# A new list order for a scheduled kernel: transposing DMAs earlier, some loads later

## The chip, the cores and the metric

The kernel runs on one NeuronCore of a Trainium2 chip. Its engines run side by side: PE (TensorE, matrix products, with PEld for loading weights), DVE (VectorE), ACT (ScalarE), POOL (GpSimd) and SP (SyncE, which here only issues DMAs). Sixteen DMA engines move data between HBM and SBUF, the on-chip memory; matrix products land in PSUM, which has eight banks of 128 x 512 float32. The metric is the device time of one execution in microseconds (us). The median of three runs of the kernel before was 200.03 us (198.92 to 200.92).

## What is computed

Two branches start from the layer norm of `x = A_q` (2048 tokens, 512 channels), and their product is added to x:

```
xn = layernorm(x)
# A: a long convolution over time, per channel, by FFT
k_shift = sum over t < 4 of k_pad[:, t:t+S] * shift_k[:, 3-t]
kv = k_shift * v
y  = irfft(rfft(pad(kv)) * rfft(pad(ssm_k)))[:S] + kv * ssm_D
s  = xn * y
# B: a gated feed-forward layer, 512 -> 1792 -> 512
h  = gelu(xn @ w_gate) * (xn @ w_up)
g  = silu(h @ w_down)
out = x + s * g
```

All tensors are bfloat16; the sums are float32.

## The kernel before

**The feed-forward branch.** The tokens are cut into four quarters q0 to q3 of 512. For each quarter the normalized rows XN are transposed to xnT (q0 and q1 on PE, q2 and q3 by a transposing DMA, line 846). Each of 14 column blocks m has a gate task (psg) and an up task (psu) of four matmuls of 128x512 each; ACT takes the gelu out of PSUM to GE (three buffers, L1137), and DVE multiplies it with the up product into HT (L1140). The down tasks (psd) multiply HT with Wd. Of q0, the blocks m = 0 and 1 go in two halves of 256 columns (L1128, L1130). The weights come as chunks g0 to g3 and u0 to u3, and Wd as Wd0 and Wd1.

**The convolution branch** is an FFT written as matrix products in two stages, with a trip to HBM between them. The filter ssm_k comes as Hn0 to Hn3. Hn0 and Hn1 are transposed on PE into HTr; Hn2 and Hn3 are first permuted by ACT (four HP copies, L609), and then the two halves HP0 and HP1 are transposed by DMA into HTD0 and HTD1 (L899). DVE adds ssm_D to one row of each (fold and foldD). Stage 1 of the filter multiplies HTr (H0 to H7) and HTD (J0 to J7) with the table F1; the results are evicted to the AST buffers, stored to HBM as ZH (H stores by ACT's queue, J stores by SP's) and loaded again as BH. Stage 1 of kv does the same: DVE makes k_shift out of the loads KK0 to KK4 and the taps SKB (which POOL copies out of SKR), chain kac and ktm, eight vector operations per quarter, the last one writing kv over V (L1005 to L1013); PE multiplies V with F1 (K0 to K7), and the evictions go through three AST slots to ZK and come back as BK. The second stage (32x32 tiles, L1028) works on BH and BK, DVE multiplies the two spectra (L1091), the inverse uses the tables MI0 and MI1 (made by ACT, m_turn at L729, and transposed by DMA at L1039), results go out as ZI, and the last y tasks read BI.

**What sets the order.** Every step is a task with a number; `S.add` gives it the engine (or a choice of two engines) and a planned duration. The string `SEQ` lists all 787 tasks in the order in which they are emitted, and a `b` behind a number takes the second engine. So each engine's instructions, and each queue's DMAs, stand in the order of that list, and each engine works in that order: what stands behind a waiting instruction on its engine waits too. Loads (planned as a queue of their own, `loads`) and the planner's `SP` tasks are both issued by SP, in one order. `Sched.run` walks the list with planned times; since order and engine are fixed by the list, its times only choose buffer slots: `Pool_.find` takes the slot of a pool (PSUM banks, AST, GE, HS, BO and so on) that is planned to be free first. `Trk` adds the semaphore waits that the data and the slots need.

Task numbers that the text uses:

| number | task | engine |
|---|---|---|
| 25, 26 | loads of Hn2, Hn3 | SP |
| 30, 28, 29, 37, 38 | loads of SKR, g2, u2, g3, u3 | SP |
| 35, 40, 44, 46 | loads of V0, V1, V2, V3 | SP |
| 43, 41, 42 | loads of KK3, Wd0, Wd1 | SP |
| 57, 58; 59, 60 | copies to HP0 out of Hn2, Hn3; to HP1 | ACT |
| 61, 62 | transposing DMAs to HTD0, HTD1 | SP |
| 64 | foldD | DVE |
| 81 | m_turn, which makes TFA and TFB | ACT |
| 122, 128, 129, 130 | J0's matmuls; J2's, its eviction, its store ZH10 | PE, PE, ACT, SP |
| 166 | first step of kac2, reads KK3 | DVE |
| 183, 184 | transposing DMAs to MI0, MI1 | SP |
| 252, 257 | K5's and K6's second matmul pair | PE |
| 406, 430, 409 | psu0_7, first reader of u2; psu0_13, a reader of u3; psg0_8 | PE |
| 433, 448 | first down tasks of rows 0 and 3 of q0 | PE |
| 467, 469 | transposes of XN5 and XN7 | PE |

Of the kernel before, what the change touches and what calls it, by code (L numbers as in the profile page):

```python
# [24 lines left out]
N_WARM = 11  # L25
ORDER = "x02 h0 h1 x22 w0 w1 h2 h3 D0 w2 s0 k0 v0 x1 w3 k1 v1 d0 d1 k2 v2 k3 v3 x2 x3"
SEQ = (
# [22 lines left out]
)  # L50
NF_BANKS = 4
ISSUE = 470.0
# [1 line left out]
W_XT, W_SW, W_BK, W_BH, W_ZI, W_BI, W_ZK, W_MI, W_G1 = 1665000, 600000, 555000, 703000, 333000, 640000, 490000, 740000, 222000  # L54
# [237 lines left out]
class Sched:  # L292
# [7 lines left out]
    SHARE_BW = 300.0  # L300
    FIRST = {"loads": 1050.0, "SP": 30500.0}
    DRAIN = 121.0
    EARLY, TAKEN, SHARED, WAIT = (0.0, 1.0), 1400.0, 46000.0, ((30000.0, 5000.0), (38000.0, 1500.0), (46000.0, 4500.0), (57000.0, 2000.0))
    LANDS = (4350.0, 5590.0, 6870.0, 8420.0, 9350.0, 10200.0)

    def __init__(self):
# [92 lines left out]
def build_kernel(nc, A_q, A_k, A_v, A_shift_k, A_ssm_k, A_ssm_D, B_w_gate, B_w_up, B_w_down, out):  # L399
    with ExitStack() as es0:  # L400
# [104 lines left out]
        S = Sched()  # L505
# [128 lines left out]
        bHP, bHTD = [[B(f"{x}{h}") for h in range(2)] for x in ("HP", "HTD")]  # L634
# [255 lines left out]
        h_perm, h_dtr = [], []  # L890
        d_htd = [dsem(f"d_htd{hf}") for hf in range(2)]
        for hf in range(2):
            for k in range(2):
                h_perm.append(op([("ACT", 2090.0)], lambda e, h, hf=hf, k=k: copy(e, h, HP[:, 8 * hf:8 * hf + 8, k, :], Hn[:, 2 + k, :].rearrange("p (a t) -> p t a", t=NT)[:, 8 * hf:8 * hf + 8, :]),
                                 r=[bHn[2 + k]], w=[bHP[hf]], rr=[R_Hn[2 + k]], ww=[R_HP[hf]]))
        for hf in range(2):
            def dtr(e, hf=hf):
                o = HTD[:, 8 * hf:8 * hf + 8, :, :].rearrange("p t k d -> p (t k) d")
                trk.dma("SP", lambda h: h.dma_start(out=o, in_=HP[:, 8 * hf:8 * hf + 8, :, :].rearrange("p t k a -> p (t k a)"), transpose=True), d_htd[hf], r=[R_HP[hf]], w=[R_HTD[hf]])  # L899
            h_dtr.append(S.add([("loads", 2900.0)], dtr, r=[bHP[hf]], w=[bHTD[hf]], nbytes=W_XT))  # L900
        HT0 = HTr[0:1, 0, :].rearrange("p (d c) -> p c d", c=2)[:, 0, :]
        HD0 = HTD[0:1, 0, :, :].rearrange("p k d -> p (k d)")
        bFold, bFoldD = B("fold"), B("foldD")
# [1 line left out]
           r=[bHD, *[bHTr[k][0] for k in range(2)]], w=[bFold], rr=[R_D, *R_HTr[0]], ww=R_HTr[0])  # L905
        op([("DVE", 420.0)], lambda e, h: h.tensor_tensor(HD0, HD0, Drow[:, 256:512], ALU.add),
           r=[bHD, bHTD[0]], w=[bFoldD], rr=[R_D, R_HTD[0]], ww=[R_HTD[0]])
# [315 lines left out]
        for j in range(6):  # L1223
# [7 lines left out]
                  r=[b2], w=[B(f"out{j}")], nbytes=262144)  # L1231
# [12 lines left out]
def bass_recurrent_scan__ssm_conv_h3__glu_gated_geglu__prompt_kernel(  # L1244
    nc: bass.Bass,
    A_q: bass.AP,
    A_k: bass.AP,
    A_v: bass.AP,
    A_shift_k: bass.AP,
    A_ssm_k: bass.AP,  # L1250
    A_ssm_D: bass.AP,
    B_x: bass.AP,
    B_w_gate: bass.AP,
    B_w_up: bass.AP,
    B_w_down: bass.AP,
    out: bass.AP,
):
    build_kernel(nc, A_q, A_k, A_v, A_shift_k, A_ssm_k, A_ssm_D, B_w_gate, B_w_up, B_w_down, out)
# [28 lines left out]
```

## Time and profile before

| | |
|---|---|
| median of three runs | 200.03 us |
| the profiled execution | 198.18 us |
| its span, first to last instruction | 196.4 us |
| PE busy in it | 188.6 us, 96% |
| DVE, ACT busy | 163.6 and 122.6 us |
| bytes moved | 49.19 MB, mean 250 GB/s |
| clock granted to PE | full speed throughout |

A row of the timeline has the start in us, the length in us, the engine (a q behind it means the engine's queue, which issues DMAs), the line, the operation, output and inputs, the shape and how many instructions were merged; the bracket is the idle time of the engine just before and what ended it. A row of the chain of waits has start, length and what was done. A row of the table by stage has the stretch, its length, for PE, PEld, DVE, ACT and POOL the busy time with the number of instructions, then PE's clock, the share of the DMA engines and GB/s. A row of the list of DMAs ends with the number of transfers, the size and the median time from issue to landing.

### The profile page before, as it was taken

To read this page: it belongs to the slowest core of one execution; us is meant where nothing else is said; L and a number is where in the kernel's file an instruction comes from. 1 tells how busy PE (TensorE), PEld (TensorE's weight loads), DVE (VectorE), ACT (ScalarE), POOL (GpSimd) and SP (SyncE) were. 2 spreads that over 40 slices of the span, in tenths; PEclk is the share of its full clock that TensorE was granted. 3 is DMA by queue.
4 is the path that set the end of the run, shared out by engine and by line. 5 is a ranking of instruction groups with operands and counts; after the bars stand their busy time and mean duration, and the time that the engine had idled before them with its cause. 6 is when DMAs were issued, how large, how long until landed. Compare 5 with 4: busy or idle time off the path is not lost.

```text
span 196.4 us, 3497 instructions
## 1 busy us (share of the span) xinstructions
PE 188.6 (96%) x1377; PEld 84.5 (43%) x1377; DVE 163.6 (83%) x249; ACT 122.6 (62%) x166; POOL 13.8 (7%) x32
## 2 busy tenths in 40 slices
PE   8899969999999999899999999999999999999993
PEld 2675425444444444334344343434333444444442
DVE  6799896999979997968689977958797986598993
ACT  5796596996988797767665655868775522430121
POOL 5322600000000000020210000000000000000000
PEclk9999999999999999999999999999999999999999
DMA  6999999199999999999999893958152433929443
GB/s 169 321 328 314 374 386 410 36 168 228 355 351 392 267 298 256 385 335 328 255 255 282 187 344 139 316 190 304 69 203 110 160 110 123 391 80 366 160 147 124
DMA packets 45958, 49.19 MB, mean 250 GB/s; under 512 B 12787, under 2 KB 39671, under 8 KB 45942
## 3 DMA queue, kind: packets, MB, share of 16 engines
q1 hardware_dynamic: 37366, 42.67, 69.7%
q10 hardware_dynamic: 8576, 6.29, 11.0%
q8 instruction: 11, 0.18, 0.4%
q14 instruction: 5, 0.04, 0.1%
HBM read 27.39 MB, written 14.68 MB: 214 GB/s over the span
## 4 chain that ended last, share of the span: by engine, by line
PE 65%; DMA 21%; ACT 7%; SPq 3%; issue 2%; DVE 1%; ACTq 0%
PE psall L618 60%; DMA Wu<-in_B_w_up_dram 8%; PE psall L1028 5%; DMA Wd<-in_B_w_down_dram 4%; DMA Wg<-in_B_w_gate_dram 4%; DMA ZK<-AST 3%; SPq L590 2%; DMA ZH<-X 2%; ACT X L609 2%; ACT GE L1137 1%; ACT HP L609 1%; ACT TFA L729 1%; ACT AST L609 1%; ACT TFB L729 1%; ACTq L590 0%
## 5 line engine op out<-in xcount | busy, mean ns | idle before, releaser
L618 PE MATMUL psall<-xnT,Wu 128*128 128x512 bf16 (+1 forms) x232 | 54.8, 372 | 1.9 <-DMA Wu<-in_B_w_up_dram 1.9
L618 PE MATMUL psall<-xnT,Wg 128*128 128x512 bf16 (+1 forms) x232 | 54.4, 372 | 0.1
L618 PE MATMUL psall<-Wd,HT 128*128 128x512 bf16 (+2 forms) x238 | 52.5, 367 | 0.3 <-DMA Wd<-in_B_w_down_dram 0.3
L1140 DVE TENSOR_TENSOR HT<-psall,GE 128x512 bf16<-128x512 f32 x54 | 36.7, 686 | 11.5 <-PE psall L618 11.5
L1137 ACT ACTIVATE GE<-psall 128x512 bf16<-128x512 f32 x54 | 30.9, 599 | 14.2 <-PE psall L618 10.6
L618 PEld LDWEIGHTS psall<-xnT,Wu 128*128 128x128 bf16 x232 | 21.9, 98 | 28.3 <-issue 2.2
L618 PEld LDWEIGHTS psall<-Wd,HT 128*128 128x128 bf16 x238 | 22.2, 98 | 26.7 <-issue 1.7
L618 PEld LDWEIGHTS psall<-xnT,Wg 128*128 128x128 bf16 x232 | 21.4, 98 | 25.6 <-issue 2.5
L609 ACT ACTIVATE HS<-psall 128x1024 bf16<-128x1024 f32 x14 | 13.9, 1024 | 6.0 <-PE psall L1028 6.0
L1011 DVE TENSOR_TENSOR KAC<-KAC,KTM 128x2048 bf16<-128x2048 bf16 x12 | 14.6, 1220 | 0.1
L1009 DVE TENSOR_TENSOR KTM<-KK,SKB 128x2048 bf16<-128x2048 bf16 x12 | 14.6, 1217 | 0.0
L609 ACT ACTIVATE KB<-psall 128x1024 bf16<-128x1024 f32 x11 | 11.1, 1026 | 5.7 <-PE psall L1028 5.7
L609 ACT ACTIVATE AST<-psall 128x1024 bf16<-128x1024 f32 x12 | 12.0, 1026 | 3.0 <-PE psall L618 2.9
L1172 ACT ACTIVATE G<-psall 128x512 bf16<-128x512 f32 (+2 forms) x5 | 2.6, 512 | 17.1 <-PE psall L618 17.1
L609 ACT ACTIVATE X<-psall 128x512 bf16<-128x512 f32 (+1 forms) x16 | 12.6, 819 | 0.7 <-PE psall L618 0.7
L1166 DVE SCALAR_TENSOR_TENSOR G<-G,psall 128x512 bf16<-128x512 bf16 x12 | 8.1, 682 | 5.7 <-ACT G L1164 5.7
L612 DVE CAST BO<-psall 128x1024 bf16<-128x1024 f32 x9 | 10.9, 1222 | 1.9 <-PE psall L1028 1.9
L1164 ACT ACTIVATE G<-psall 128x512 bf16<-128x512 f32 x12 | 6.8, 595 | 8.0 <-PE psall L618 8.0
L609 ACT ACTIVATE BO<-psall 128x1024 bf16<-128x1024 f32 x7 | 7.2, 1024 | 7.3 <-PE psall L1028 7.2
L821 DVE BATCH_NORM_STATS2 stats<-X 128x6 f32<-128x512 bf16 x16 | 10.5, 678 | 1.0 <-DMA X<-in_A_q_dram 1.0
L1091 DVE TENSOR_TENSOR HW<-KB,HW 128x1024 bf16<-128x1024 bf16 x16 | 10.9, 683 | 0.0
L1091 DVE TENSOR_TENSOR HS<-KB,HS 128x1024 bf16<-128x1024 bf16 x16 | 10.9, 684 | 0.0
(84 smaller groups left out, 176.3 us busy)
## 6 DMA issues: line engine op xcount, KB each, us to landing
BH<-ZH SPq DMA_DIRECT2D x8, 512.0 KB, 6.6
HW<-HS SPq DMA_DIRECT2D x16, 256.0 KB, 3.5
BK<-ZK SPq DMA_DIRECT2D x8, 512.0 KB, 5.1
ZI<-BO ACTq DMA_DIRECT2D x16, 256.0 KB, 2.5
BI<-ZI SPq DMA_DIRECT2D x8, 512.0 KB, 4.1
ZK<-AST SPq DMA_DIRECT2D x6, 512.0 KB, 5.3
Hn<-in_A_ssm_k_dram SPq DMA_DIRECT2D x4, 512.0 KB, 8.4
KK<-in_A_k_dram SPq DMA_DIRECT2D x4, 512.0 KB, 11.1
```

Source lines behind the costliest of these rows:

```text
L609: return h.activation(o, i, ACTF.Copy, scale=scale)
L612: return h.tensor_copy(o, i)
L618: return h.matmul(o, lhsT=l, rhs=r, start=st, stop=sp)
L821: t_stats[t] = op([("DVE", 670.0)], lambda e, h, t=t: h.bn_stats(stats[:, t, :], X[:, t, :]), r=[bX[q][t % 4]], w=[bst[t]], rr=[R_X[t]], w ...
L1009: op([("DVE", dur)], lambda e, h, j=j, m=m: h.tensor_tensor(KTM[:, m.slot, :, :], kk(j), sk(j), ALU.mult), r=need + [bSKB[j], a], w=[m], r ...
L1011: op([("DVE", dur)], lambda e, h, m=m: h.tensor_tensor(KAC[:, a.slot, :, :], KAC[:, a.slot, :, :], KTM[:, m.slot, :, :], ALU.add), r=[m], ...
L1028: trk.op("PE", lambda h: h.matmul(ps(s, i)[b, :], lhsT=wt(col)[a, :], rhs=data(col)[a, :], start=n < 16, stop=n >= len(todo) - 16, tile_po ...
L1091: return hd.tensor_tensor(o, flat(KB, kb[h]), o, ALU.mult)
L1137: op([("ACT", act(512))], lambda e, h: h.activation(GE[:, g.slot, :], bank(pg), ACTF.Gelu_apprx_tanh), r=[pg], w=[g], rr=lambda: R_bank(pg ...
L1140: op([("DVE", dve(512, 1))], lambda e, h: h.tensor_tensor(HT[:, q % 2, m, :], bank(pu), GE[:, g.slot, :], ALU.mult), r=[pu, g], w=[bHT[q][m]],
L1164: op([("ACT", act(n))], lambda e, h, g=g, pc=pc: h.activation(g, pc(), ACTF.Tanh, scale=0.5), r=[p], w=[bt], rr=lambda p=p: R_bank(p), ww= ...
L1166: op([("DVE", dve(512, 1))], lambda e, h, g=g, pc=pc: h.scalar_tensor_tensor(out=g, in0=g, scalar=1.0, in1=pc(), op0=ALU.add, op1=ALU.mult ...
```

## The change

No instruction is added or taken away. The list `SEQ` is replaced, with twelve evictions moved from DVE to ACT and eight from ACT to DVE; two planner constants and the planned duration of the two HTD transposes change.

```diff
 SEQ = (
-    "17 18 19 20 21 22 36 0 3 2 11 8 4 12 5 1 6 7 9 65 66 50 10 67 73 68 74 13 49 75 82 52b 112 107 51 76 113 83 87 86b 102 71 23 72 69 24 79 54 "
...
+    "0 2 3 1 17 5 18 19 8 7 11 50 4 9 12 10 65 13 49 6 66 73 67 68 51 74 52b 82 75 54 112 76 86b 83 20 117 56 21 87 71 53 118 72 119 102 69 70 79 "
+    "120 369 371 121 22 55b 377 77 370 80 85 78 379 84 372 89 14 93 88 103 36 23 24 378 107 113 108 114 380 373 31 459 25 30 375 381 455 460 15 "
...
-    EARLY, TAKEN, SHARED, WAIT = (0.0, 1.0), 1400.0, 46000.0, ((30000.0, 5000.0), (38000.0, 1500.0), (46000.0, 4500.0), (57000.0, 2000.0))
+    EARLY, TAKEN, SHARED, WAIT = (0.0, 1.0), 1050.0, 46000.0, ((30000.0, 5000.0), (38000.0, 1500.0), (46000.0, 4500.0), (57000.0, 2800.0), (75000.0, 1000.0))
...
-            h_dtr.append(S.add([("loads", 2900.0)], dtr, r=[bHP[hf]], w=[bHTD[hf]], nbytes=W_XT))
+            h_dtr.append(S.add([("loads", 3900.0)], dtr, r=[bHP[hf]], w=[bHTD[hf]], nbytes=W_XT))
```

`TAKEN` is what a store costs the loads behind it in the plan, `WAIT` what is added to a transfer's planned landing by its time. What the new list does to SP's queue, from its tenth DMA on (the first nine and the last two are the same; "store" marks a store):

| | SP's queue |
|---|---|
| before | KK0 halo, SKR, g2, halo, Hn2, KK1, zero row, D, u2, g3, u3, Hn3, KK2, V3, V0, KK3, HTD1, HTD0, Wd1, Wd0, MI0, V2, V1, store ZH13, store ZK0, store ZH15, KK4, store ZH11, store ZK1, store ZH8, store ZH14, X2, MI1, ... |
| after | KK0 halo, Hn2, SKR, halo, g2, KK1, zero row, u2, Hn3, g3, D, u3, KK2, V0, HTD0, V3, HTD1, V1, MI0, MI1, KK3, Wd1, store ZH10, V2, Wd0, store ZH12, KK4, X2, store ZH8, store ZH9, G1, store ZK0, store ZK1, ... |

On PE, the gate and up tasks of q0 and q1, the stage-1 tasks and the down tasks of q0 are permuted with them: task 430 has 31.5 us of PE's time ahead of it instead of 26.1 (from the span's start, with PE never waiting), the first down task 55.6 instead of 51.7, J0 53.9 instead of 55.2. On ACT the four HP copies stand 20th, 23rd, 33rd and 41st (counted from 0) instead of 26th, 32nd, 44th and 41st, in the order 57, 59, 58, 60 instead of 57, 59, 60, 58. On POOL, rstd of q1 comes behind one SKB copy instead of two. Behind task 257 the order of q1's end, q3 and q2 changes in places; BK, BH, HW and the two xnT transposes keep theirs but for swaps of neighbours.

41 rows, old and new, of the table SEQ are left out of this document.

## The prediction

> **What bounds the kernel now.** I read the page first: engine shares, the 40 slices, then the timeline of PE for its idle times.
>
> ```profile
> span 196.4 us, 3497 instructions
> PE 188.6 (96%) x1377; PEld 84.5 (43%) x1377; DVE 163.6 (83%) x249; ACT 122.6 (62%) x166; POOL 13.8 (7%) x32
> DMA  6999999199999999999999893958152433929443
> ```
>
> TensorE works for 188.6 of 196.4 us, and the change neither adds nor removes an instruction. So what the change can win is PE's idle time: 7.8 us. The timeline of PE says where it lies (the bracket is the idle time before a row and what ended it):
>
> ```profile
> 0.97 4.60 PE L618 MATMUL psall<-AST 128*128 128x512 bf16 x11 [0.97 <-DVE AST L671]
> 25.09 1.90 PE L618 MATMUL psall<-xnT,Wu 128*128 128x512 bf16 x8 [0.79 <-DMA Wu<-in_B_w_up_dram]
> 29.41 1.89 PE L618 MATMUL psall<-xnT,Wu 128*128 128x512 bf16 x8 [1.11 <-DMA Wu<-in_B_w_up_dram]
> 55.54 1.02 PE L618 MATMUL psall<-Wd,HT 128*128 128x512 bf16 x4 [0.26 <-DMA Wd<-in_B_w_down_dram]
> 82.18 0.60 PE L618 MATMUL psall<-V,F 128*128 128x512 bf16 x2 [0.94 <-ACT AST L609]
> ...
> 187.60 5.81 PE L618 MATMUL psall<-Wd,HT 128*128 128x512 bf16 x40
> ```
>
> After 82 us PE has no wait until its end at 193.4 (the last row); the 3.0 us behind that are the last evictions and the last store, whose tasks stand in the same order before and after. PE starts at 0.97. **Four waits can be won, 3.1 us together**: u2, u3 (up weights), Wd0 and an AST slot.
>
> To follow a new order I use a due time for each PE task: when it would start if PE began at 0.97 and never waited, from the spacing of these rows:
>
> ```profile
> 58.13 1.03 PE L618 MATMUL psall<-xnT,Wu 128*128 128x512 bf16 x4
> 58.99 0.59 PE L618 MATMUL psall<-HTD,F 128*128 128x512 bf16 x2
> 59.42 2.10 PE L618 MATMUL psall<-Wd,HT 128*128 128x512 bf16 x9
> 61.36 0.59 PE L618 MATMUL psall<-HTD,F 128*128 128x512 bf16 x2
> ```
>
> So 0.86 for a gate or up task, 0.43 for a stage-1 pair, 0.216 for each down matmul; half of these for half the columns. Due times before: u2's first reader (task 406) 23.0, u3's (430) 26.1, Wd0's (433) 51.7, task 257 77.2. Started: 25.09, 29.41, 55.54, 82.18. **Lateness 2.1, 3.3, 3.8, 5.0**; the other 2.7 up to the end come behind 82 us, where both lists alternate 48 times between full and 32x32 matmuls, and I carry them over.
>
> **Part 1: the first loads.** On SP's queue load 25 (Hn2) moves from behind 30 (SKR) and 28 (g2) to ahead of both; 26 (Hn3) moves ahead of 37 and 38 (g3, u3).
>
> ```profile
> 18.52 1.93 POOL L986 COPY SKB<-SKR 128x512 bf16<-128x512 bf16 x2 [6.81 <-DMA SKR<-in_A_shift_k_dram]
> 20.42 0.24 POOL L831 TENSOR_SCALAR mv<-mv 128x4 f32<-128x4 f32 x1
> 20.75 1.05 POOL L832 TENSOR_TENSOR mv<-mv,NHALF 128x4 f32<-128x4 f32 x1
> 21.76 2.09 ACT L609 ACTIVATE HP<-Hn 128x1024 bf16<-128x1024 bf16 x1 [2.33 <-DMA Hn<-in_A_ssm_k_dram]
> 24.36 0.41 DVE L835 TENSOR_SCALAR XN<-X,mv 128x512 bf16<-128x512 bf16 x1
> ```
>
> SKR had landed by 18.5 and Hn2, two loads later, by 21.7: 1.6 us a load. After: Hn2 at 18.5, SKR 20.1, g2 21.7; u2 has the same bytes ahead of it and stays at 25.1; u3 gets one more, 29.3 + 1.5 = 30.8. PE now asks for u2 at due time 24.1 and for u3 at 31.5, so with any lateness over 1 us **both waits, 1.9 us, go**.
>
> What is late next: POOL does one SKB copy (0.97), then rstd of the second quarter (1.4), then XN5 and XN7 (0.4 each): 20.1 + 0.97 + 1.4 + 0.8 = 23.3. PE has their transposes (467, 469) at due 20.9 and 21.1, behind 409, which needs g2 at 21.7. They end at 23.6 against due 21.3: lateness 2.3. Add 0.1 for what is reordered in the first 13 us (the transpose of XN2 is asked for 0.9 earlier and its data comes about 0.5 earlier; hidden in the 2.3 unless SKR is early). So **lateness 2.4 instead of 3.3** behind u3: -0.9. Bounds: 1.6 if SKR lands first in 18.5, 3.3 if the early ZH7 store (now the first on ACT's queue, before ge0_1_0) delays these loads by its own time, half a load's.
>
> **Part 2: the HP copies and the transposing DMAs.**
>
> ```profile
> L1137 ACT ACTIVATE GE<-psall 128x512 bf16<-128x512 f32 x54 | 30.9, 599 | 14.2 <-PE psall L618 10.6
> ...
> 35.56 2.10 ACT L609 ACTIVATE HP<-Hn 128x1024 bf16<-128x1024 bf16 x1
> 38.54 2.08 ACT L609 ACTIVATE HP<-Hn 128x1024 bf16<-128x1024 bf16 x1
> 42.95 1.59 ACT L729 ACTIVATE TFA<-TF 128x512 bf16<-128x512 bf16 x2
> 37.69 8.54 SPq L899 DMA_TRANSPOSE HTD<-HP  x2
> 36.00:39.00 3.00, 3.00 (x16) 1.35 (x15) 3.00 (x5) 3.00 (x4) 0.00 (x0) 1.00 0.00 0
> 39.00:51.00 12.00, 12.00 (x57) 5.41 (x56) 11.58 (x13) 10.04 (x14) 0.00 (x0) 1.00 1.17 221
> 51.00:59.20 8.20, 7.94 (x37) 3.44 (x36) 6.61 (x9) 7.18 (x10) 0.00 (x0) 1.00 1.10 357
> ```
>
> The stretches end with DMA share and GB/s. From 36 to 39 no byte moved; then the DMA engines are full up to 59. HP0's second copy (task 58, at 38.54) goes ahead of eleven ACT tasks (some 8 us: one HP copy of 2.1 and ten evictions of 0.6 or, for two wider ones, somewhat more) and behind one, and ACT loses part of its wait of 2.33 for Hn2: done near 31.5. HTD0's issue follows there. V0, now the last load ahead of it, has two loads less ahead than the last one before 36.0, at 1.5 each (0.52 MB at 357 GB/s): the loads run to 33.1, and **the idle gap of 3 us is filled**. HP1 (60) ends near 37.5, so HTD1 follows without a gap. The m_turn copies (81) have as much work ahead as before, so MI0 can be issued from 44.5.
>
> But the order behind the transposes is the other one. Before: KK3, V3 and V0 had landed by 36, then HTD1, HTD0, Wd1, Wd0. After: HTD0, V3, HTD1, V1, MI0, MI1, KK3, Wd1, ZH10, V2, Wd0. DMA time, from the rows:
>
> - HTD twice: 12.0 less four ZH stores of 0.73 (half a load) = 9.1.
> - V3, V1, KK3, V2 at 1.47: 5.9.
> - Wd twice and MI0: 8.2 less the loads of V2 and V1 = 5.3.
> - MI1, never alone in the trace: between 0.2 (what MI0 leaves of the 5.3 beside two Wd of 2.57) and 2.3 (half an HTD, being half its size); I take 2.0, near the other transpose's rate.
> - Five ACT stores and ZH10: 4.4.
>
> Sum 26.7 from 33.1: **Wd0 lands at 59.8**. PE's first reader is 448, due 55.6, with lateness 2.4 at 58.0: a wait of 1.8 plus 0.1 for the start, lateness 4.3, against 3.8 before.
>
> [...]
>
> SP is the other bound on Wd0, since all of these are issued in one order:
>
> ```profile
> 40.64 5.58 SPq L899 DMA_TRANSPOSE HTD<-HP  x1
> 47.97 4.51 SPq L1039 DMA_TRANSPOSE MI<-TFA  x1
> 64.54 1.50 SPq L1039 DMA_TRANSPOSE MI<-TFB  x1
> 47.31 8.09 DMA Wd<-in_B_w_down_dram
> 46.50 1.22 DVE L1005 TENSOR_TENSOR KAC<-KK,SKB 128x2048 bf16<-128x2048 bf16 x1
> 59.20 1.22 DVE L1013 TENSOR_TENSOR V<-KAC,V 128x2048 bf16<-128x2048 bf16 x1 [1.53 <-DMA V<-in_A_v_dram]
> 74.83 6.19 DMA ZK<-AST
> ...
> ZK<-ASX SPq DMA_DIRECT2D x1, 512.0 KB, 5.0
> ```
>
> A MI transpose holds SP for 1.5 to 4.5. I take the mean, 3.0 each: SP is free for KK3 at 50.5, and KK3 lands near 55. DVE reaches its reader (166, at 46.50 before, now with four HT tasks and three kac1 steps more and one HT task less ahead, 5.2 us) at 52 and waits 3 us; before, it waited 1.53 for V1 without stopping PE. Queued behind 166 on DVE is the fold of HTD0 (64, the next task there), which PE's first J task (122, due 53.9, at 56.3) needs: 55 + 1.2 + 0.3 = 56.5. That is 0.2, inside the wait for Wd0. ZH10 waits on SP for AJ2's eviction (its matmuls are due 49.2, so near 53.4 on ACT), so Wd0 is issued near 54.5, which 59.8 allows.
>
> **Part 3: the AST slot.** The wait at 82.18 is ACT waiting for a ZK store of 6.19 us. After, PE comes to task 257 at 77.2 + 4.3 = 81.5. The store's last input (252) has due 68.6 instead of 67.9; with 4.3 and two evictions of 1024 columns in ACT's queue, near 1.0 each (0.6 is the price of 512), the store is issued near 75.2, lands between 80.2 (5.0) and 81.4 (6.19), and 257 starts between 81.5 and 82.5: I take 82.0. **Lateness 4.8 instead of 5.0.**
>
> **Part 4: everything else.**
>
> ```profile
> 165.33 9.40 SPq L590 DMA_DIRECT2D BI<-ZI  x5
> 173.35 1.89 PE L618 MATMUL psall<-BI,G 128*128 128x512 bf16 x8
> BI<-ZI SPq DMA_DIRECT2D x8, 512.0 KB, 4.1
> ```
>
> Twelve evictions go from DVE to ACT and eight back; the q3 and q2 tasks, BK, HW and output DMAs are permuted. PE never waited there, xnT3 and xnT2 keep their places, and the last inverse is due 153.0 instead of 152.5 with the first y task at 165.0 instead of 165.8. The first BI landed near 169.4, 3.9 us ahead of its reader; 2.6 of that cover are left. I count it as nothing; if the ZI stores come more than 2.6 late, PE waits for the rest. `TAKEN`, `WAIT` and 3900 act only through the choice of buffer slots, since the list fixes order and engine; bounds -0.3 to +1.0, the upper the size of one wait at 82.18.
>
> **Sum.** -0.9 (loads) +1.4 (Wd0: 1.9 in place of 0.5) -0.7 (AST: 0.5 in place of 1.2) = **-0.2 us**: span 196.2. The profiled execution took 198.18 with a span of 196.4, the median was 200.03; on the median I forecast **199.8**.
>
> **Rivals.**
>
> *The transposes come early enough (faster).* If MI0 and MI1 hide beside the loads and HTD takes less than 4.5 each, Wd0 lands by 58 and nothing is added there; with the AST wait gone as well, lateness is 2.4 to 2.8 at 257 in place of 5.0: -2.2, **197.8**. For it: the filled gap. Against it: 221 GB/s. [...]
>
> *SP is held (slower).* If each MI takes 4.5 to issue, as MI0 did, KK3 is issued at 53.5, V2 near 55 and Wd0 at 55.5; with 8.09 to land that is 63.6. PE's lateness becomes 63.7 - 55.6 = 8.1 in place of 5.0 at 257: +3.1, **203.1**; DVE's seven-us wait for KK3 adds up to 0.5. It decides from a landing of Wd0 behind 62.6. For it: a MI just behind other transfers took 4.51. Against: MI1 took 1.50.
>
> *The change does not act.* The new list fixes queue order, so the order must change; that times stay is the forecast's own band.
>
> **How the numbers follow.** Forecast 0.5, early transposes 0.2, SP held 0.3 (three things must arrive behind two transposes, so its share is above the other's). A measurement of this kernel tells about 1% (2 us) from no change. Range 197.6 to 203.5: both rivals' points. Faster by over 1% 0.2, within 0.5, slower 0.3.
>
> **What would show it.** The PE waits for Wu gone; a short one for XN or POOL's rstd near 23; HTD's first issue near 31.5 and DMA share above zero throughout 33 to 39; a PE wait for Wd near 58 to 60; DVE waiting for KK. The prediction is wrong if PE waits for something else for more than 1 us, such as a PSUM bank behind ACT between 35 and 46, or if PE idles behind 85 us.

## The result and the profile after

The changed kernel takes 202.72 us (median; 201.74 to 203.27), the kernel before beside it 199.56 us: **slower by 1.5%**, ratio 1.0149 with a 95% interval of 1.0108 to 1.0190. Forecast was no change (199.8 from 200.03, range 197.6 to 203.5). The profiled execution took 203.27 us against 198.18 before, so the profiled pair differs by 5.1 us, more than the medians (3.2): 198.18 lies 1.4 under the median of its kernel, and 203.27 is the longest of the six. What follows accounts for the 5.1 of that pair. Ratios, here and below, leave out executions over 1.5% above the fastest of their kernel and differ somewhat from the quotients of the medians (most with ZH10 moved alone: 1.0061 against 1.0105).

The page of the changed kernel, the lines that answer to those shown of before:

```profile
span 201.5 us, 3511 instructions
PE 191.9 (95%) x1377; PEld 85.8 (43%) x1377; DVE 159.1 (79%) x245; ACT 126.5 (63%) x170; POOL 12.3 (6%) x32
PEclk9999999999996799999999999999999999999999
DMA  6999998995999487998999962898161534959407
```

The work of the four engines is the same 3201 instructions; the 14 more in the first line are of kinds that are not counted as busy. The same 1377 matmuls keep PE busy 191.9 us instead of 188.6, and the row of the granted clock has a dip, a 6 and a 7, that was not there before. The idle gap of the DMA engines at 36 us is filled; a dent (5) stands at 45 to 50 us instead. The timeline of PE, with all its waits and the rows behind the last one:

```profile
0.97 4.88 PE L618 MATMUL psall<-AST 128*128 128x512 bf16 x11 [0.97 <-DVE AST L671]
9.35 0.61 PE L618 MATMUL psall<-HTr,F 128*128 128x256 bf16 x4 [0.20 <-ACT HTr L609]
11.82 0.40 PE L854 MATMUL psall<-ident,XN 128*128 128x128 bf16 x4 [0.18 <-DVE XN L835]
21.74 1.02 PE L618 MATMUL psall<-xnT,Wg 128*128 128x512 bf16 x4 [0.21 <-DMA Wg<-in_B_w_gate_dram]
23.21 0.40 PE L854 MATMUL psall<-ident,XN 128*128 128x128 bf16 x4 [0.23 <-DVE XN L835]
57.28 0.59 PE L618 MATMUL psall<-HTD,F 128*128 128x512 bf16 x2 [1.06 <-DVE HTD L906]
58.92 0.60 PE L618 MATMUL psall<-HTD,F 128*128 128x512 bf16 x2 [0.19 <-DVE HT L1140]
62.93 1.86 PE L618 MATMUL psall<-Wd,HT 128*128 128x512 bf16 x4 [3.40 <-DMA Wd<-in_B_w_down_dram]
...
70.09 1.03 PE L618 MATMUL psall<-Wd,HT 128*128 128x512 bf16 x4
```

PE now idles 6.4 us in waits of this kind; before it was 4.6 (the four of the prediction, the 0.97 at the start, and 0.5 for Hn at 6.1). That is +1.9; with +3.3 of busy time it makes +5.2, the 5.1 of the span. Most of the +3.3 is the clock: four Wd matmuls took 1.86 at 62.93 and 1.03 at 70.09. The stretches of the span around it (the column before the last two is the granted clock):

```profile
61.00:62.00 1.00, 0.00 (x0) 0.00 (x0) 1.00 (x2) 1.00 (x2) 0.00 (x0) 0.73 1.13 386
62.00:68.00 6.00, 5.07 (x12) 1.75 (x13) 6.00 (x6) 1.42 (x3) 0.00 (x0) 0.50 0.77 269
68.00:69.00 1.00, 1.00 (x5) 0.44 (x4) 0.96 (x2) 0.41 (x1) 0.00 (x0) 0.85 0.00 0
```

A mean of 0.73, six of 0.50 and one of 0.85 are 0.54 + 6 + 0.30 = **6.8 us at half the clock**, begun 1.9 us into the wait for Wd0 (59.53 to 62.93), at 61.46. PE worked in 5.4 of them, so it did 2.7 us less. Of the other 0.6, the first eleven matmuls hold 0.3 (4.88 instead of 4.60); the rest isn't located.

Why Wd0 is late stands in SP's queue, and in what SP waited for between 40 and 60 us (engine, line, cause: total, times, longest):

```profile
44.44 1.25 SPq L1039 DMA_TRANSPOSE MI<-TFA  x1
48.75 1.23 SPq L1039 DMA_TRANSPOSE MI<-TFB  x1
50.03 0.58 SPq L590 DMA_DIRECT2D KK<-in_A_k_dram  x1
...
53.10 0.39 SPq L590 DMA_DIRECT2D ZH<-X  x1
53.53 0.51 SPq L590 DMA_DIRECT2D V<-in_A_v_dram  x1
54.08 0.65 SPq L590 DMA_DIRECT2D Wd<-in_B_w_down_dram  x1
```

```profile
SPq L1039 <- DMA MI<-TFA: 2.8, 1, 2.8
SPq L590 <- ACT X L609: 2.0, 1, 2.0
```

From 39.4 to 44.4 SP stood before MI0, whose input ACT's m_turn makes; the prediction had that. Behind it, SP stands still twice more. MI1 waits 2.8 us until MI0 has landed, since both transposes use the semaphore `d_g1`, on which a second DMA waits for the first. Then the store ZH10 waits 2.0 us for its input, the eviction of AJ2, with V2 and Wd0 queued behind it. The table by stage shows the DMA engines in that time, 0.70 busy at 144 GB/s, and full before and after:

```profile
36.00:39.00 3.00, 3.00 (x15) 1.36 (x14) 3.00 (x4) 3.00 (x5) 0.00 (x0) 1.00 0.95 245
...
45.00:52.00 7.00, 7.00 (x34) 3.18 (x33) 6.16 (x8) 5.09 (x9) 0.00 (x0) 1.00 0.70 144
52.00:60.00 8.00, 6.28 (x28) 2.35 (x26) 4.32 (x7) 4.71 (x7) 0.00 (x0) 1.00 0.99 319
```

The chain of waits has Wd0's transfer as one piece, and DVE's timeline the step ahead of the fold:

```profile
54.08 8.72 DMA Wd<-in_B_w_down_dram
```

```profile
55.72 1.23 DVE L1005 TENSOR_TENSOR KAC<-KK,SKB 128x2048 bf16<-128x2048 bf16 x1 [3.68 <-DMA KK<-in_A_k_dram]
56.86 0.27 DVE L906 TENSOR_TENSOR HTD<-HTD,Drow 1x256 bf16<-1x256 bf16 x1
```

Issued at 54.08, Wd0 lands at 62.8. KK3 keeps DVE waiting 3.68 us, and the fold of HTD0 behind it costs PE the 1.06 at 57.28.

### The profile page after: what moved, and what is told of

Its sections match the earlier page's. It is cut to its first block, busy times and chain, and to the rows that moved or that the text cites. A ratio compares the mean times of both kernels' runs of the same rounds, so it can differ in the third digit from the quotient of the medians.

```text
span 201.5 us, 3511 instructions
## 1 busy us (share of the span) xinstructions
PE 191.9 (95%) x1377; PEld 85.8 (43%) x1377; DVE 159.1 (79%) x245; ACT 126.5 (63%) x170; POOL 12.3 (6%) x32
## 4 chain that ended last, share of the span: by engine, by line
PE 80%; DMA 10%; SPq 5%; issue 1%; ACT 1%; DVE 1%; DVEq 0%; ACTq 0%
PE psall L618 75%; DMA KK<-in_A_k_dram 6%; PE psall L1028 5%; SPq L590 5%; DMA Wd<-in_B_w_down_dram 4%; ACT X L609 1%; PE psall L854 0%; DVE G L1175 0%; DVE G L1174 0%; ACT G L1172 0%; ACT GE L1137 0%; DVE XN L835 0%; DVEq L173 0%; ACT AST L609 0%; ACTq L173 0%
## 5 line engine op out<-in xcount | busy, mean ns | idle before, releaser
L618 PE MATMUL psall<-xnT,Wg 128*128 128x512 bf16 (+1 forms) x232 | 56.7, 376 | 0.2 <-DMA Wg<-in_B_w_gate_dram 0.2
L618 PE MATMUL psall<-Wd,HT 128*128 128x512 bf16 (+2 forms) x238 | 53.5, 374 | 3.4 <-DMA Wd<-in_B_w_down_dram 3.4
L618 PE MATMUL psall<-xnT,Wu 128*128 128x512 bf16 (+1 forms) x232 | 55.5, 372 | 0.0
L1137 ACT ACTIVATE GE<-psall 128x512 bf16<-128x512 f32 x54 | 31.6, 599 | 22.8 <-PE psall L618 18.0
L1140 DVE TENSOR_TENSOR HT<-psall,GE 128x512 bf16<-128x512 f32 x54 | 36.2, 681 | 7.3 <-PE psall L618 3.8
L618 PEld LDWEIGHTS psall<-xnT,Wg 128*128 128x128 bf16 x232 | 22.0, 99 | 26.6 <-issue 3.5
L609 ACT ACTIVATE BO<-psall 128x1024 bf16<-128x1024 f32 x12 | 11.8, 1022 | 7.2 <-PE psall L1028 7.2
L609 ACT ACTIVATE HS<-psall 128x1024 bf16<-128x1024 f32 x13 | 12.8, 1022 | 4.5 <-PE psall L1028 3.6
L618 PE MATMUL psall<-V,F 128*128 128x512 bf16 x32 | 9.3, 395 | 0.0
```

The lines of the kernel that those rows point to most:

```text
L609: return h.activation(o, i, ACTF.Copy, scale=scale)
L618: return h.matmul(o, lhsT=l, rhs=r, start=st, stop=sp)
L1137: op([("ACT", act(512))], lambda e, h: h.activation(GE[:, g.slot, :], bank(pg), ACTF.Gelu_apprx_tanh), r=[pg], w=[g], rr=lambda: R_bank(pg ...
L1140: op([("DVE", dve(512, 1))], lambda e, h: h.tensor_tensor(HT[:, q % 2, m, :], bank(pu), GE[:, g.slot, :], ALU.mult), r=[pu, g], w=[bHT[q][m]],
```

## Experiments

My theory after the two traces: SP's order makes Wd0 and KK3 late (two holds, MI1 and ZH10), and PE's idling then costs clock on top. The rivals: the transposes' own time in the DMA engines is what counts; or PE's permuted order costs; or the clock fell for some reason other than PE's idling. Every time is the median, with its ratio to the kernel before on the same chip. Where a list is reordered so that the planner would choose other buffer slots, the slots of the unmoved kernel are written into the file, which shifts line numbers by 26 or 27.

**MI1 on its own semaphore.**

```diff
-            def g1(e, out_ap=out_ap, in_ap=in_ap, rr=rr, ww=ww):
-                trk.dma(e, lambda h: h.dma_start(out=out_ap, in_=in_ap, transpose=True), d_g1, r=[rr], w=[ww])
+            def g1(e, out_ap=out_ap, in_ap=in_ap, rr=rr, ww=ww, d=d_g1 if ww is not R_MI[1] else dsem("d_mi1")):
+                trk.dma(e, lambda h: h.dma_start(out=out_ap, in_=in_ap, transpose=True), d, r=[rr], w=[ww])
```

> The changed kernel with a semaphore of its own for MI1, so that its issue no longer waits on SP for MI0's landing; list, slots and everything else as they are. Theory 1 (SP is held: MI1's issue waits for MI0 from 45.7 to 48.75, and all loads behind it start late): KK3 is issued near 47 in place of 50.03 and lands near 52 to 53, DVE's wait for KK3 falls from 3.7 to under 1, PE's wait of 1.06 for the fold goes; Wd0 still stands behind ZH10, which is ready at 53.1, so it lands near 61 and PE's wait falls from 3.4 to about 2; time 2 us below the changed kernel's 202.7. Theory 2 (DMA time sets Wd0's landing, whoever holds SP): Wd0 lands at 62 to 63 as before and the time stays within 0.7 us of 202.7.

Measured: 204.46 us (203.68 to 205.72), ratio 1.026 [1.018, 1.034]. The hold by MI1 is gone, and the 2 us of Theory 1 are not won. SP's queue, and PE's two large waits:

```profile
47.07 1.68 SPq L1039 DMA_TRANSPOSE MI<-TFB  x1
48.79 0.86 SPq L590 DMA_DIRECT2D KK<-in_A_k_dram  x1
...
54.63 0.38 SPq L590 DMA_DIRECT2D ZH<-X  x1
```

```profile
23.68 1.02 PE L618 MATMUL psall<-xnT,Wg 128*128 128x512 bf16 x4 [1.58 <-DMA Wg<-in_B_w_gate_dram]
...
64.72 1.86 PE L618 MATMUL psall<-Wd,HT 128*128 128x512 bf16 x4 [5.24 <-DMA Wd<-in_B_w_down_dram]
```

KK3 goes out at 48.79 and the wait for the fold disappears. But SP now stands before ZH10 from 50 to 54.63, and Wd0 is issued at 55.61 and lands at 64.6. ZH10 came 1.5 later than in the changed kernel because PE itself was late: 1.9 at the wait for g2 (23.68 instead of 21.74), lost there and in the first 13 us, which the edit doesn't touch; why this kernel was slow there in its profiled execution stays open, and so does whether that explains the whole 1.7 over the changed kernel.

**ZH10 behind Wd0.** The list's 130 moves:

```diff
-483 232 130 44 135 167 474 41 233
+483 232 44 135 167 474 41 130 233
```

> The changed kernel with the store ZH10 issued behind Wd0 instead of ahead of V2 and Wd0; same slots. Theory 1: V2 and Wd0 are issued near 51.2 and 51.8 in place of 53.5 and 54.1; KK3's landing (55.7) and PE's wait for the fold stay as they are, Wd0 lands 0.7 (the store's DMA time) to 2.3 earlier, PE's wait falls from 3.4 to between 1.1 and 2.7; time 0.7 to 3 us below 202.7, the larger if the clock no longer falls. Theory 2: only the store's own DMA time is gained, 0.7 us.

Measured: 201.62 us (199.0 to 202.69), ratio 1.0061 [1.0008, 1.0114]. Wd0 is issued 1.6 earlier, at 52.44, and lands only 0.35 earlier; the chain of waits and PE's timeline:

```profile
52.44 10.00 DMA Wd<-in_B_w_down_dram
```

```profile
62.57 1.02 PE L618 MATMUL psall<-Wd,HT 128*128 128x512 bf16 x4 [2.61 <-DMA Wd<-in_B_w_down_dram]
```

MI1 still holds KK3, Wd1, V2 and Wd0 together, which then go out between 50.73 and 52.44 into DMA engines that are full (1.03 to 1.17 busy at 352 to 401 GB/s from 59 to 63 us). PE's wait of 2.61 is in Theory 1's range, at its long end.

**Both holds undone, the transposes kept early.** Both edits above at once.

> The changed kernel with both holds undone and the transposes kept early: MI1 on a semaphore of its own, ZH10 behind Wd0. Theory (the holds, not the bytes of the transposes, make Wd0 late): Wd0 is issued near 50 and lands near 58.5 to 59.5; PE waits 0.5 to 1.5 for it, the fold of HTD costs under 0.5, no fall of the clock; 199.5 to 200. Rival (the transposes' own time on the DMA engines is what counts): Wd0 lands near 62 as with ZH10 alone moved, 201.6.

Measured: 197.68 us (197.15 to 197.96), ratio 0.9932 [0.9908, 0.9957]; run again on another chip, it took 197.66, ratio 0.9927 [0.9904, 0.9951].

> The changed kernel with MI1 on its own semaphore and ZH10 behind Wd0, once more, beside the run with V2 moved: PE waits 1.4 to 1.7 for Wd0, 197.7, 0.9 to 1.6 under the kernel before.

SP's queue, the chain and PE's timeline of the first of the two:

```profile
47.24 0.81 SPq L616 DMA_DIRECT2D KK<-in_A_k_dram  x1
...
49.18 0.75 SPq L616 DMA_DIRECT2D Wd<-in_B_w_down_dram  x1
53.02 1.55 SPq L616 DMA_DIRECT2D ZH<-X  x2
```

```profile
49.18 10.12 DMA Wd<-in_B_w_down_dram
```

```profile
59.44 1.02 PE L644 MATMUL psall<-Wd,HT 128*128 128x512 bf16 x4 [1.57 <-DMA Wd<-in_B_w_down_dram]
```

This settles the main question. With the transposes in place and only SP's two waits gone, Wd0 lands at 59.3, the mean clock is 0.998, and by the ratios 2.1% of the changed kernel's time is gone (1.0149 to 0.9932), some 4.3 us, more than my theory expected. The permuted order of PE and the moved evictions are in this kernel too, so they don't cost it. **It was the waits in the issuing queue that cost, not the transposes' bytes.** The two holds are in series for Wd0, which is why either edit alone gives little or nothing:

| ratio to the kernel before | ZH10 ahead of V2 and Wd0 | ZH10 behind Wd0 |
|---|---|---|
| MI0 and MI1 early, one semaphore | 1.0149 (the change) | 1.0061 |
| MI0 and MI1 early, two semaphores | 1.026 | 0.9932 |
| MI0 and MI1 behind KK4 and X2 | 1.0167 | 0.9967 |

**The transposes moved back.** MI0 (183) behind KK4 (45), MI1 (184) behind X2 (47), first with ZH10 left ahead of V2 and Wd0:

```diff
-509 183 423 162 424 184 519
+509 423 162 424 519
...
-516 45 485
+516 45 183 485
...
-140 47 131
+140 47 184 131
```

> The changed kernel with its two MI transposes alone moved on SP's queue (MI0 behind KK4, MI1 behind X2); ZH10 stays ahead of V2 and Wd0; buffer slots as in the changed kernel. Theory (two separate holds of SP: MI1's wait for MI0 makes KK3 late, ZH10's wait for AJ2 makes Wd0 late): KK3 is issued near 40 and lands near 47, DVE's wait of 3.7 for KK and PE's 1.06 for the fold of HTD go; Wd0 is still issued behind ZH10 near 54.5, but into emptier DMA engines, lands near 58.5 to 59.5, PE waits 0.5 to 1.5 for it, the clock keeps above 0.95; about 199.6 us. Rival (only the hold by the transposes matters): as with both moved, 198.8. Rival (ZH10's hold decides alone, Wd0 takes its 8 us anyway): Wd0 lands at 62.5, PE waits over 3 us and the clock falls, 202 to 202.7.

Measured: 202.34 us (201.49 to 202.89), ratio 1.0167 [1.0128, 1.0205]; my theory expected 199.6, and the rival that ZH10 decides alone was right. The chain and PE's timeline:

```profile
54.43 7.88 DMA Wd<-in_B_w_down_dram
```

```profile
62.45 1.02 PE L644 MATMUL psall<-Wd,HT 128*128 128x512 bf16 x4 [4.15 <-DMA Wd<-in_B_w_down_dram]
```

KK3 was issued at 39.84 and no longer matters, the DMA engines had run nearly empty before (0.21 busy at 63 GB/s from 50.0 to 54.4 us), and still Wd0 took 7.88 us from its issue, beside V2, ZH12, KK4 and MI0. In this and the rows above Wd0 takes **some 8 to 10 us from issue to landing** (7.88 to 10.12), always beside other transfers; after the emptier stretch it was only 0.8 shorter than in the changed kernel (8.72). It is no fixed price: in the kernel before, Wd1, a load of the same size (896 KB), landed 6.6 us after its issue.

With ZH10 behind Wd0 as well:

> The changed kernel with MI0 issued behind KK4, MI1 behind X2 and ZH10 behind Wd0; same slots. Theory 1: KK3, Wd1, V2 and Wd0 are issued from 39 on without a wait and land by 53; no PE wait for the fold or for Wd0, no clock drop; lateness at task 257 near 2.5 to 3.5 in place of 9.9, span 194 to 195.5, time near 196 to 197, below the kernel before by 1.2 to 1.8%. Theory 2 (DMA time): Wd0 lands at 59.8 less the 2 to 3 us of the MI transposes and the store, so near 57, no wait either, but then DVE or the AST slots take part of it back: time 198 to 200. If neither is right, and the loss came from the permuted PE order, the time stays near 202.

Measured: 198.75 us (198.35 to 199.18), ratio 0.9967 [0.9939, 0.9994], not the 196 to 197 of Theory 1 but in the range of Theory 2. No wait for Wd, KK or the fold is left and the clock stays at full speed, but the stores and the late transposes now crowd SP from 54 to 74 us, and PE waits for ACT, which at the first and the last of these rows waits itself (1.20 and 1.69 us) for a store to empty its buffer:

```profile
66.22 0.60 PE L644 MATMUL psall<-V,F 128*128 128x512 bf16 x2 [0.59 <-ACT G L635]
70.30 1.90 PE L644 MATMUL psall<-Wd,HT 128*128 128x512 bf16 x8 [0.45 <-ACT AST L635]
82.50 0.61 PE L644 MATMUL psall<-V,F 128*128 128x512 bf16 x2 [1.24 <-ACT AST L635]
```

Whether the transposes are better early, once they hold nothing, isn't told apart: the intervals of 0.9932 and 0.9967 overlap.

**PE kept busy in the wait.** The changed kernel with 16 matmuls of 128x512, whose results are overwritten, ahead of the first Wd0 task:

```diff
+                            if q == 0 and jt == 3 and m0 == 0:
+                                for _ in range(N_FILL):
+                                    trk.op("PE", lambda h: mm(h, pc(), F1[:, 0, :], xnT[:, 1, 0, :, :].rearrange("p k c -> p (k c)"), True, True), ..., w=R_bank(p), accum=True)
```

> The changed kernel with 16 more matmuls of 128x512 on PE (3.45 us, into the bank of the first down task of row 3 of q0, which that task then overwrites) just ahead of its wait for Wd0, so that PE is not idle there; nothing else is changed. If the halved clock between 61.5 and 68 comes from PE standing idle: the clock stays at full, PE's lateness behind that task stays near 7.3 in place of 9.9, and the time falls by 2 to 2.6 us to about 200.3, though PE has 3.4 us more to do. If the clock falls for another reason (load, chance), it falls here too and the time stays at 202.7 or above.

Measured: 201.19 us (200.45 to 202.19), ratio 1.0096 [1.0065, 1.0127], with more work on PE than the changed kernel. The timeline of PE:

```profile
59.87 3.63 PE L619 MATMUL psall<-xnT,F 128*128 128x512 bf16 x16
63.33 1.03 PE L619 MATMUL psall<-Wd,HT 128*128 128x512 bf16 x4
```

The first Wd matmuls follow the fill at 63.33, 0.4 us after Wd0 has landed (62.9), and take 1.03 instead of 1.86. The clock fell because PE idled: with the same order and the same late Wd0 it stays at 0.999 over the span, and at 0.998 to 1.0 in all ten executions. By the ratios the gain is 0.5%, some 1.1 us where 2 to 2.6 were expected, with intervals that just overlap; the changed kernel's one execution at full clock (201.74) lies beside it.

**Part 1 alone.** The kernel before with its first loads in the changed order, down to u3:

```diff
-KK0 halo, SKR, g2, halo, Hn2, KK1, zero row, D, u2, g3, u3, Hn3, ...
+KK0 halo, Hn2, SKR, halo, g2, KK1, zero row, u2, Hn3, g3, D, u3, ...
```

> The kernel before with Part 1 of the change alone: its first loads in the order of the changed kernel down to u3, all else and the buffer slots as before. Theory (the 1.1 us that Part 1 wins early are swallowed by the next gate): the PE waits for Wu (0.79 and 1.11) go and short ones for Wg or XN below 0.7 come near 22; PE comes to Wd0 some 1 us earlier, Wd0 lands as before near 55.4, and PE's wait there grows from 0.26 to 0.8 to 1.4; the AST wait near 82 stays near 1; time within 0.4 of the kernel before, 199.5. Rival (the win is kept): HTD and Wd0 move forward with it, 198.4.

Measured: 200.59 us (199.67 to 202.03), ratio 1.0077 [1.0046, 1.0107]: slower, where I expected no change; also the eight of its twelve executions with the clock at full took 199.7 to 200.8 us, above the 199.0 of the kernel before beside it. PE's timeline and the clock behind it:

```profile
30.19 1.86 PE L645 MATMUL psall<-xnT,Wg 128*128 128x512 bf16 x4 [2.21 <-DMA Wg<-in_B_w_gate_dram]
```

```profile
31.00:33.00 2.00, 2.00 (x6) 0.59 (x5) 0.00 (x0) 0.85 (x2) 0.00 (x0) 0.50 1.03 417
```

Hn3 now goes ahead of g3, and ACT's stores ZH6 and ZH7, issued at 15.6 and 16.0, get between: g3 lands at 30.05, in the changed kernel at 27.8. There, and with both holds undone, the list puts the second and the third ZH store behind the HP copies, at 20.6 and 26.2 in the latter's trace. So the order of the loads seems to pay only together with the later stores on ACT's queue. That the stores are the cause is read from the landings; it wasn't tried alone.

**V2 behind Wd0, ZK5 ahead of X3.** On the version with both holds undone, to win the rest of the wait for Wd0 and to keep the AST slot free:

```diff
-483 232 44 135 167 474 41 130 233
+483 232 135 167 474 41 44 130 233
...
-253 245 247 246 452 48 644 248 435 440 436 260 645 255 254 437
+253 254 245 247 246 452 48 644 248 435 440 436 260 645 255 437
```

> The changed kernel with both holds undone (MI1 on its own semaphore, ZH10 behind Wd0) and two more moves on SP's queue: V2 behind Wd0, ZK5 ahead of the X3 load. Theory (Wd0 is late by what is queued ahead of it in the DMA engines): Wd0 lands one load, 1.3 to 1.5 us, earlier, near 58; of PE's wait of 1.57 there 0 to 0.4 is left; no AST wait over 0.6 near 82, since ZK5 has one load less ahead of it; 196.2 to 197.0. Rival (the win is lost again at the AST slot, as in the run that moved all three): a wait of about 1 near 82 and 197.2 to 197.8.

Measured: 198.06 us (197.4 to 199.41), ratio 0.9945 [0.9921, 0.9969]: no better than the 197.7. PE's timeline, and DVE's:

```profile
58.98 1.02 PE L644 MATMUL psall<-Wd,HT 128*128 128x512 bf16 x4 [0.69 <-DMA Wd<-in_B_w_down_dram]
82.45 1.04 PE L644 MATMUL psall<-xnT,Wu 128*128 128x512 bf16 x4 [1.03 <-DVE G L1192]
```

```profile
80.91 0.69 DVE L847 BATCH_NORM_STATS2 stats<-X 128x6 f32<-128x512 bf16 x1 [3.74 <-DMA X<-in_A_q_dram]
```

0.9 of the wait for Wd0 goes (1.57 to 0.69) and 1.03 comes back at 82 us: the X3 load, now behind ZK5, is issued at 74.91 instead of 71.97 and keeps DVE waiting 3.74 us instead of 0.86 at the statistics of q3, and a step that PE needs is queued behind them. Neither theory had that.

**ZK5 ahead of X3 alone**, in the kernel before:

```diff
-246 48 248 451 447 254 185
+246 254 48 248 451 447 185
```

> The kernel before with ZK5 issued ahead of the X3 load on SP's queue and nothing else moved. Theory (the AST wait near 82 is the time that the X3 load takes ahead of ZK5 in the DMA engines): the wait of 0.94 falls under 0.3 and the time by 0.6 to 0.9, 198.3 to 198.6. Rival (the store is issued when its input is ready and takes its 6 us anyway): no change, 199.2.

Measured: 198.75 us (197.82 to 200.74), ratio 0.9992 [0.9962, 1.0023]: no difference that this shows, though the AST wait of 0.94 is gone from PE's timeline. A wait of 0.31 for DVE has come at 84.94.

**All the left waits at once.** The run with the three moved behind Wd0, and on top of it g2 ahead of Hn2 (25 behind 28), ZK1 behind ZH12 (234 behind 136), ZK0 ahead of G1 (229 ahead of 182), ZK5 ahead of X3, and MI1 on its own semaphore; SP's queue at the first of these:

```diff
-KK0 halo, Hn2, SKR, halo, g2, KK1, ...
+KK0 halo, SKR, halo, g2, Hn2, KK1, ...
```

> The changed kernel with MI0, MI1 and ZH10 moved behind Wd0 as in the run that moved all three, and with the waits that were left there taken on: g2 ahead of Hn2, MI1 on a semaphore of its own, ZK1 issued behind ZH12, ZK0 ahead of G1, ZK5 ahead of the X3 load. Theory (the waits of 0.63 for Wg, 0.59 for G, 0.45 and 1.24 for AST are each a store or load that stood behind another on SP): at least 1.5 of these 2.9 us go, 196.0 to 197.3. Rival (the DMA engines are full up to 110 us and each order only moves the wait): 198.4 to 199.

Measured: 201.74 us (199.93 to 203.46), ratio 1.0118 [1.0072, 1.0165], far from the 196.0 to 197.3 of the theory. ACT's timeline and PE's:

```profile
22.36 2.05 ACT L635 ACTIVATE HP<-Hn 128x1024 bf16<-128x1024 bf16 x1 [5.10 <-DMA Hn<-in_A_ssm_k_dram]
```

```profile
24.73 1.89 PE L644 MATMUL psall<-xnT,Wg 128*128 128x512 bf16 x4 [2.91 <-ACT GE L1154]
```

Hn2 lands at 22.3 instead of 18.0, ACT stands before its first HP copy for 5.1 us with the next gelu eviction queued behind it, and PE waits 2.91 for that eviction. The wait of 0.63 for g2 was the cheap side of this. The clock was at half behind it (6.8 us of the span), so the other moves can't be judged by this run. The profiled execution is the longest of the six (203.46); how much of the median this wait makes isn't shown.

## Why the prediction was wrong

**Part 1 held, as far as the lateness goes.** The waits for u2 and u3 are gone, a short one for g2 and one for XN came (0.21 and 0.23). PE reached J0's matmuls at 56.22 (57.28 less the wait), due 53.9: lateness 2.3, predicted 2.4. The reason that I gave, the order of the loads, was not enough: by the run with this part alone they win nothing without something else in the new list, probably the later ZH stores on ACT's queue. Of those stores my working named only the early ZH7.

**Part 2's bound by SP is the step that failed.** HTD0 was issued at 30.3 (predicted 31.5), the gap was filled, the two MI transposes held SP from 44.44 to 50.03 (predicted 44.5 to 50.5, at 3.0 each), and KK3 landed at 55.7 (55). The reason for the hold was not the transposes' length, as I had it: they took 1.25 and 1.23 to issue, and the rest was MI1 waiting for MI0's landing. In the run with both holds undone, Wd0 landed at 59.3, against the 59.8 of the DMA sum; so the sum may be right for a queue without holds, but its terms aren't shown one by one, and with V2 (1.47 in the sum) behind Wd0 the landing came only 0.5 to 1.0 earlier, at 58.8 (59.3 and 59.9 in the two runs with V2 ahead). What failed is "Wd0 is issued near 54.5, which 59.8 allows". I had the issue right (54.08) and quoted a row with 8.09 us from Wd0's issue to its landing, used it in the rival, and left it out of the forecast, where Wd0's landing was taken from the DMA sum alone: 54.5 + 8.09 is 62.6, and it was 62.8. Lateness behind it is 62.93 - 55.6 = 7.3 instead of 4.3. The fold made PE wait 1.06 and not 0.2, since KK3 landed 0.7 later than taken; as Wd0 ends later still, that costs nothing by itself.

**A term was missing: the clock.** At 70.09 PE was 9.9 late (task 443, due 60.2). The 2.6 between are the half clock, for which nothing in the profile of before stood, whose longest wait was 1.11. The forecast had priced a wait at its length. The changed kernel's executions differ by this: the mean clock over the span was 0.98 to 0.99 in five, and full in the one that took 201.74.

**Part 3 turned around.** With PE 9.9 late, the ZK store is long landed and the AST wait of 0.94 is gone, where I had kept 0.5. Part 4 held: no wait behind 82 us. In all, the span's miss of 5.3 (196.2 to 201.5) is +3.0 for Wd0, +2.6 for the clock, -0.5 for AST and 0.2 of small things.

**The rivals.** "SP is held" was the true mechanism, with the right deciding point (a landing of Wd0 behind 62.6; it was 62.8) but with other parts: it had PE 8.1 late by the wait alone, where the wait gave 7.3 and the clock 2.6 more, so that its 203.1 lies near the 202.7 in part by luck. "The transposes come early enough" was false for the change; that both holds undone gave 197.68, near its 197.8, is luck of the base: there the kernel before took 199.01 and the win was 1.3 us, not 2.2, with Wd0 at 59.3 and not by 58.

## What to carry to other kernels

A queue that issues in order is a resource like the engines: for every store or transposing DMA moved ahead of a load, ask when its input is ready and whether it shares a semaphore with a DMA still in flight, and charge that wait to everything behind it, plus the load's own time from issue to landing. Two such waits in series hide each other, so undo both before judging either. A wait of TensorE can cost more than its length: here each of the six profiled waits of 2.21 to 5.24 us came with half clock, 3.4 or 6.8 us of it, though not in every execution of these kernels, and those of up to 1.6 us did not.

## What the runs showed of the hardware that was not expected

**The half clock came as 3.4 or 6.8 us.** In the profiled executions, waits of up to 1.6 us (1.57 with both holds undone) left the clock at full speed. With ZH10 moved alone, and with Part 1 alone, it was at half for 3.4 us behind waits of 2.61 and 2.21; in the changed kernel (3.40), with MI1's semaphore alone (5.24), and with all the left waits taken on (2.91), for 6.8; but with the transposes moved back (4.15) for 3.4 again. A drop is not unknown to the kernel before either: 2 of its 69 executions beside these runs show 0.99, by what wait isn't known. The stretches with ZH10 moved alone:

```profile
63.00:64.00 1.00, 1.00 (x6) 0.52 (x5) 1.00 (x2) 0.00 (x0) 0.00 (x0) 0.93 1.06 410
64.00:67.00 3.00, 3.00 (x9) 1.07 (x8) 2.17 (x2) 1.62 (x2) 0.00 (x0) 0.50 0.98 299
67.00:68.00 1.00, 1.00 (x6) 0.37 (x5) 0.99 (x1) 0.00 (x0) 0.00 (x0) 0.87 1.98 214
```

0.14 + 3 + 0.26 is 3.4 us, begun 1.3 us after PE was back at work; in the changed kernel the drop began while PE still waited, 1.9 us into the 3.40. The same kernel is hit in some executions and not in others: with ZH10 moved alone, seven at a mean clock of 0.99 took 201.4 to 202.7 us, and three at 0.997 to 1.0 took 199.0 to 200.6. The length of the wait alone doesn't order them: 2.91 us brought 6.8 us of half clock, and 4.15 us brought 3.4. What sets the 3.4 us, and when a drop begins, no run shows.
